# Gated decode step on one core: output weights in two halves with one transpose each, second feed-forward matrix ahead of the first keys

## Chip, cores and metric

The kernel runs on one core of one Trainium2 chip. The metric is device time in microseconds (us) of one execution: the median of the runs shown. The profile is of one further execution, whose span runs from its first to its last instruction.

## What is computed

One decode step for two sequences (B = 2, one token each, D = 640): attention of 32 heads over a cache of 4096 keys and values of 128 elements each, a feed-forward block with SiLU (F = 1728), and a sigmoid gate that mixes the two. All is float32.

```python
q = (x @ wq).reshape(B, 1, 32, 128).transpose(0, 2, 1, 3)
p = softmax(einsum("bhqd,bhkd->bhqk", q, k_cache) * 128 ** -0.5)
a = einsum("bhqk,bhkd->bhqd", p, v_cache).transpose(0, 2, 1, 3).reshape(B, 1, 4096) @ wo
b = silu(x @ w1) @ w2
g = sigmoid((x * gate_w).sum(-1, keepdims=True))
return g * a + (1 - g) * b
```

Keys and values are 134 MB each and everything else together is under 30 MB, so nearly all bytes that the kernel reads are read once, for one use.

## The kernel before

**Items and slabs.** The 32 heads are taken four at a time (Q = 4, HQ = 8 groups); a group and a sequence make an item, 16 in all. The keys of an item are one slab of 64 KB in each of 128 partitions (8.39 MB), its values another. Three slots of that size (`slabs`, line 52) hold everything large that is in flight: keys, values, query weights, feed-forward weights, output weights.

**Order of the loads.** `stream` (lines 80 to 88) is the list of slot contents in order: two blocks of weights (`wq` 0; `wq` 1, which also holds w1 and a few small inputs), then keys and values alternately. From item 7 on the keys of an item stand ahead of the values of the item before, because a block `mid` was put in after the keys of item 6. `mid` holds the output weights of groups 0 and 1 and the second feed-forward matrix; a last block `end` holds the output weights of groups 2 to 7. All these DMAs are issued by SP, in the order of the list. A block is issued when the block three places ahead of it has been marked as used up (`pump`, `spend`, lines 126 to 138); SP then waits until the engines have really read that slot. Everything that SP issues waits behind such a wait.

**One item.** `products` multiplies keys by the query, 60 of 128 columns of heads and positions on GpSimd (POOL, line 343), 68 on VectorE (DVE, line 346), in place. `scores` (line 354) sums over the 128 elements on DVE; after it the slot of the keys is spent. `peak` finds the maximum, `weights` (line 369, ScalarE) takes the exponential. One step later, beside the next item's keys, TensorE (PE) sums the weights (`total`), DVE inverts the sum (`invert`), and `values` (line 395) multiplies weights and values: 32 matmuls on four column strips, each recorded as two instructions, because the data are float32.

**From values to output.** `combine` (line 407) scales the result and keeps of each row the quarter that belongs to its head (`osb`, 128 x 4 x 128). A matmul with the 0/1 matrix `pick` (line 417) puts the rows of both sequences of a group in place in a PSUM tile `orow`. After the second sequence, `turn` (lines 425 to 429) sums over the four quarters (`row`) and transposes 128 x 128 elements to `oP`, four stationary operands for `project`. `project` (line 433) multiplies them by the group's output weights, four rows of 640 per partition. `accumulate` (line 222) has two targets: `early`, two strips of 320 columns, and `late`, four strips of 160; `merge` (line 235) copies `early` out on ScalarE and adds it into `late` with four small matmuls.

**Where the parts stand.** `middle` (line 443) runs after the values of item 5, on PE: the projections of groups 0 and 1 and `ffn_out`, with the contents of `mid`. Groups 2 to 7 are projected after the loop (line 474): 2 to 5 into `early`, 6 and 7 into `late`. The last values are loaded in two halves, and the last output weights in seven DMAs of which the last brings one row of 640 per partition. Then `ot` is copied (line 478) and written out by SP.

**Order on each engine.** The engines run their instructions in the order in which the program writes them (`manual_schedule`, line 60): nothing is moved by a scheduler. The loop is the one thing that sets it:

```python
for i in range(N + 1):
    if i < N:
        products(i)
    if i >= 1:
        total(i - 1); invert(i - 1); values(i - 1)
    if i == MID + 1:
        middle()
    if i < N:
        scores(i); peak(i); weights(i)
        ...
    if i >= 1:
        combine(i - 1)
        ...
```

Of the kernel before, what the change touches and what calls it, by code (L numbers as in the profile page):

```python
# [8 lines left out]
F32 = mybir.dt.float32  # L9
# [6 lines left out]
def tile_gated_decode(  # L16
# [12 lines left out]
    nc = tc.nc  # L29
# [18 lines left out]
    LEAD = 224  # L48
# [13 lines left out]

    ident = lead.tile([P, LEAD], F32, name="ident")[:, :P]

# [4 lines left out]
    MID = 5  # L69
# [5 lines left out]
    WO_MID = 2  # L75
    WO_AT = {}
    for grp in range(HQ):
        WO_AT[grp] = ("mid", W2T_AT + HD + grp * Q * D) if grp < WO_MID else ("end", (grp - WO_MID) * Q * D)
# [13 lines left out]

    def load_wo(grp, t):
        at = WO_AT[grp][1]
        src = wo[grp * QD : (grp + 1) * QD, :].rearrange("(p n) d -> p (n d)", n=Q)
        cuts = (0, Q * D - D, Q * D) if grp == HQ - 1 else (0, Q * D)
        for c0, c1 in zip(cuts, cuts[1:]):
            nc.sync.dma_start(t[:, at + c0 : at + c1], src[:, c0:c1])

    def load(what, n, t):  # L100
        if what in ("k", "v"):
# [3 lines left out]
            step = SLAB // 2 if (what, n) == ("v", N - 1) else SLAB  # L105
            for c in range(0, SLAB, step):
                nc.sync.dma_start(t[:, c : c + step], src[:, c : c + step])
# [7 lines left out]
        elif what == "mid":  # L115
            for grp in range(WO_MID):
                load_wo(grp, t)
# [4 lines left out]
        else:  # L122
            for grp in range(WO_MID, HQ):
                load_wo(grp, t)
# [33 lines left out]
    pick = const.tile([P, P + HB], F32, name="pick")  # L158
    nc.vector.memset(pick, 0.0)
    nc.vector.reduce_sum(pick[:, HB : P + HB : 32], sel.rearrange("p (q c) -> p q c", c=4), axis=AX.X)  # L160
# [9 lines left out]
    xz = const.tile([P, J, 32], F32, name="xz")  # L170
# [9 lines left out]
    hT = const.tile([P, FR, HB + 1], F32, name="hT")  # L180
# [35 lines left out]
    LAST = HQ - 2  # L216
# [3 lines left out]
    total_of = {"early": Q * LAST + FR + 1, "late": Q * (HQ - LAST) + 1}  # L220
# [66 lines left out]
    def ffn_out():  # L287
        t = T["mid", 0]
        for n in range(FR):
            accumulate(hT[:, n, :], t[:, n * D : (n + 1) * D])  # L290
# [8 lines left out]
        count["early"] += 1  # L299

# [103 lines left out]
    def combine(i):  # L404
        hq, b = items[i]
        osb = work.tile([P, 4, DH], F32, tag="osb", name="osb")
# [8 lines left out]
        if b == 0:  # L415
            PO[hq] = ps_r.tile([P, 4, DH], F32, name="orow")
        nc.tensor.matmul(  # L417
            PO[hq].rearrange("p c d -> p (c d)"),
            pick[:, HB * (1 - b) : HB * (1 - b) + P],
            osb.rearrange("p c d -> p (c d)"),  # L420
            start=(b == 0),
            stop=(b == B - 1),
        )

    def turn(hq):
        OP[hq] = const.tile([P, Q, 32], F32, name=f"oP{hq}")
        row = work.tile([P, DH], F32, name="row", bufs=1)
        nc.vector.reduce_sum(row, PO[hq].rearrange("p c d -> p d c"), axis=AX.X)  # L428
        nc.vector.transpose(OP[hq], row.rearrange("p (i n) -> p n i", n=Q))
# [3 lines left out]
    def project(grp):  # L433
        where, at = WO_AT[grp]
        w = T[where, 0][:, at : at + Q * D]
        to = "early" if grp < LAST else "late"
        for n in range(Q):
            lhsT = OP[grp][:, n, :] if count[to] == 0 else OP[grp][:, n, : HB + 1]
# [3 lines left out]

    def middle():
        for grp in range(WO_MID):
            project(grp)
# [57 lines left out]
```

## Time and profile before

| what | us |
|---|---|
| median of 3 runs | 700.46 |
| lowest and highest of them | 699.23, 700.59 |
| profiled execution | 700.36 |
| its span | 698.5 |
| DVE, POOL, PE busy | 469.4, 265.7, 224.7 |

Busy time is the sum of the durations of an engine's instructions; issuing DMAs is not counted. PE's time can be counted twice over where matmuls overlap, and PE's clock is granted between half and full speed. A page's lists give, for a group of instructions, the line of the kernel, the engine, what is written and read, the shape, the count, then busy time and mean duration, then the idle time of the engine ahead of them and what ended it. A timeline row is: start, duration, engine, line, operation, count, and in brackets the idle time ahead of it and its releaser. "SPq" is a DMA being issued, not being carried out; when it has landed shows in the time "to landing" or in the start of what waited for it.

### The profile page before, as it was taken

Reading aid. Unit: us, or ns where it says so; the run is one execution under the profiler, and the core shown is the slowest. Engines: PE = TensorE matmul, PEld = TensorE weight load, DVE = VectorE, ACT = ScalarE, POOL = GpSimd, SP = SyncE. Lnnn points to the kernel's source line nnn. Section 1 sums busy time; section 2 is a strip of 40 time slices with the busy share of each in tenths; the row PEclk is TensorE's granted clock in tenths of the full one; section 3 lists DMA queues with packets and bytes.
Section 4 is the critical chain, followed back from the end, with each engine's and each line's share of the span. In section 5 each row is a group of like instructions: output and inputs, shape, how many; then the busy total and the mean of one; then the engine's idle time right before and its main releaser. Section 6 shows DMA issues by size and latency. Waiting matters only on the chain.

```text
span 698.5 us, 3649 instructions
## 1 busy us (share of the span) xinstructions
PE 224.7 (32%) x1516; PEld 73.4 (11%) x1516; DVE 469.4 (67%) x215; ACT 37.8 (5%) x143; POOL 265.7 (38%) x27
## 2 busy tenths in 40 slices
PE   1630050605032150752240506050321406060477
PEld 1210010101010010210010102010100102010113
DVE  2016949394967869496949597695949495786901
ACT  0000000101010100101010101000010101010010
POOL 1006244270907153353618080624426080715300
PEclk9985565756657575877575757566565757566689
DMA  9999999999999999999999999999999999999995
GB/s 410 408 454 424 420 455 439 420 428 440 443 428 432 424 448 435 413 446 439 424 440 432 439 428 440 428 435 435 436 432 432 435 424 448 428 440 424 425 416 248
DMA packets 6803, 298.51 MB, mean 427 GB/s; under 512 B 759, under 2 KB 895, under 8 KB 1154
## 3 DMA queue, kind: packets, MB, share of 16 engines
q1 hardware_dynamic: 6780, 298.26, 98.8%
q8 instruction: 12, 0.20, 0.1%
q14 instruction: 5, 0.04, 0.0%
q10 hardware_dynamic: 6, 0.01, 0.0%
HBM read 298.26 MB, written 0.01 MB: 427 GB/s over the span
## 4 chain that ended last, share of the span: by engine, by line
DMA 60%; DVE 24%; PE 13%; another core or an unknown queue 1%; ACT 0%; issue 0%; SPq 0%; DVEq 0%; ACTq 0%
DMA k<-in_A_k_cache_dram 34%; DMA v<-in_A_v_cache_dram 20%; DVE s L354 15%; PE pv L395 10%; DVE k L346 8%; DMA wq<-in_B_w_dram 5%; PE acc L226 2%; PE orow L417 1%; PE hr L257 1%; DVE osb L407 0%; ACT pz L369 0%; PE tot L380 0%; DVE rg L388 0%; DVE m L359 0%
## 5 line engine op out<-in xcount | busy, mean ns | idle before, releaser
L343 POOL TENSOR_TENSOR k<-k,qsb 128x7680 f32<-128x7680 f32 x16 | 262.8, 16422 | 386.4 <-DMA k<-in_A_k_cache_dram 386.4
L354 DVE TENSOR_REDUCE s<-k 128x68 f32<-128x8704 f32 (+1 forms) x32 | 276.3, 8677 | 0.0
L346 DVE TENSOR_TENSOR k<-k,q 128x8704 f32<-128x8704 f32 x16 | 147.5, 9221 | 136.5 <-DMA k<-in_A_k_cache_dram 126.4
L395 PE MATMUL pv<-v,pz 128*32 128x512 f32 x1024 | 145.2, 730 | 247.9 <-DMA v<-in_A_v_cache_dram 247.9
L395 PEld LDWEIGHTS pv<-v,pz 128*32 128x32 f32 x1024 | 36.5, 131 | 342.7 <-issue 226.7
L417 PE MATMUL orow<-osb,pick 128*128 128x512 f32 x32 | 22.8, 800 | 117.4 <-DVE osb L407 117.4
L369 ACT ACTIVATE pz<-s,nb 32x128 f32<-32x128 f32 x64 | 25.5, 398 | 585.2 <-DVE nb L363 584.6
L407 DVE SCALAR_TENSOR_TENSOR osb<-pv,rg,own 128x512 f32<-128x512 f32 x16 | 12.0, 748 | 21.3 <-PE pv L395 21.2
L276 DVE STREAM_TRANSPOSE turned<-hr 128x416 f32<-128x416 f32 (+1 forms) x2 | 0.8, 414 | 29.4 <-PE hr L265 29.4
L380 PE MATMUL tot<-rs,fold 128*128 128x1 f32 x32 | 5.8, 251 | 43.9 <-ACT pz L369 43.9
L417 PEld LDWEIGHTS orow<-osb,pick 128*128 128x128 f32 x32 | 5.8, 226 | 127.1 <-DVE osb L407 127.1
L331 PE MATMUL q<-qrow,spread 128*128 128x128 f32 x32 | 7.2, 359 | 26.1 <-DVE tot L385 17.8
L314 PE MATMUL qr<-wq,xz 128*32 128x512 f32 x80 | 11.5, 745 | 8.7 <-DMA wq<-in_A_wq_dram 8.7
L428 DVE TENSOR_REDUCE row<-orow 128x128 f32<-128x512 f32 x8 | 5.5, 692 | 11.6 <-PE orow L417 11.6
L380 PEld LDWEIGHTS tot<-rs,fold 128*128 128x128 f32 x32 | 7.2, 235 | 55.3 <-ACT pz L369 52.3
L226 PE MATMUL acc<-mid,hT 128*17 128x320 f32 x52 | 10.0, 556 | 7.6 <-DMA mid<-in_B_w_dram 7.6
L369 ACT ACTIVATION_READ_ACCUMULATOR pz<-s,nb 32x1 f32 x64 | 11.8, 184 | 0.0
L226 PE MATMUL acc<-end,oP 128*17 128x320 f32 (+2 forms) x128 | 11.2, 367 | 0.0
L331 PEld LDWEIGHTS q<-qrow,spread 128*128 128x128 f32 x32 | 5.4, 240 | 33.0 <-issue 22.9
L478 DVE COPY ot<-acc 128x160 f32<-128x160 f32 x1 | 0.3, 324 | 11.0 <-PE acc L226 11.0
L257 PE MATMUL hr<-wq,xz 128*32 128x416 f32 x40 | 5.6, 681 | 3.7 <-DMA wq<-in_B_w_dram 3.7
L197 DVE COPY xz<-xT 128x10 f32<-128x10 f32 x1 | 0.2, 168 | 9.1 <-PE xT L189 9.1
(59 smaller groups left out, 69.0 us busy)
## 6 DMA issues: line engine op xcount, KB each, us to landing
v<-in_A_v_cache_dram SPq DMA_DIRECT2D x2, 4096.0 KB, 38.3
end<-in_A_wo_dram SPq DMA_DIRECT2D x5, 1280.0 KB, 21.3
wq<-in_B_w_dram SPq DMA_DIRECT2D x1, 4320.0 KB, 37.2
mid<-in_B_w_dram SPq DMA_DIRECT2D x1, 4160.0 KB, 26.8
mid<-in_A_wo_dram SPq DMA_DIRECT2D x2, 1280.0 KB, 17.4
wq<-in_A_wq_dram SPq DMA_DIRECT2D x1, 2048.0 KB, 26.5
end<-in_A_wo_dram SPq DMA_DIRECT2D x1, 960.0 KB, 27.0
end<-in_A_wo_dram SPq DMA_DIRECT2D x1, 320.0 KB, 27.3
```

The source lines that it names most:

```text
L226: nc.tensor.matmul(dst[32 * n : 32 * n + m, :], lhsT, w[:, n * width : (n + 1) * width], start=(count[to] == 0), stop=(count[to] == total_ ...
L257: nc.tensor.matmul(rows[32 * c : 32 * c + 32, :QF], xz[:, j, :], w[:, j, c * QF : (c + 1) * QF], start=(j == 0), stop=(j == J - 1),)
L314: nc.tensor.matmul(ps[u][32 * q : 32 * q + 32, :], xz[:, j, :], w[:, u * half : (u + 1) * half, q, :], start=(j == 0), stop=(j == J - 1),)
L331: nc.tensor.matmul(qps[hq][:, b, :], spread[:, b, :], qrow[:, hq, :], start=True, stop=True)
L343: nc.gpsimd.tensor_mul(k[:, CV:, :], k[:, CV:, :], qsb[hq][:, b, None, :].to_broadcast([P, C - CV, DH]))
L346: nc.vector.tensor_mul(k[:, :CV, :], k[:, :CV, :], qps[hq][:, b, None, :].to_broadcast([P, CV, DH]))
L354: nc.vector.reduce_sum(S[i][:, c0:c1], k[:, c0:c1, :], axis=AX.X)
L369: nc.scalar.activation(pz[i % 2][lo:hi, :, 4 * q : 4 * q + 4], S[i][lo:hi].rearrange("p (g c) -> p g c", c=4), AF.Exp, bias=M[i][lo:hi], s ...
L380: nc.tensor.matmul(t[:, :1], fold.rearrange("p a q c -> p (a q c)"), R[i], start=True, stop=True)
L395: nc.tensor.matmul(PV[i][32 * q : 32 * q + 32, :], pz[i % 2][:, gr, :], v[:, gr, :], start=(gr < 4), stop=(gr >= NG - 4),)
L407: nc.vector.scalar_tensor_tensor(osb, PV[i].rearrange("p (c d) -> p c d", d=DH), R[i], own[:, :, None].to_broadcast([P, 4, DH]), op0=ALU.mult,
L417: nc.tensor.matmul(PO[hq].rearrange("p c d -> p (c d)"), pick[:, HB * (1 - b) : HB * (1 - b) + P], osb.rearrange("p c d -> p (c d)"), star ...
```

## The change

- `w2`, the second feed-forward matrix, becomes a block of its own, third in the list, ahead of the first keys; `ffn_out` runs right after `ffn_in`. The blocks that follow come one place later in the rotation of three slots.
- The output weights become two blocks, `wo` 0 and 1, each half of them: 16 rows of 640 per partition (40 KB). `wo` 0 stands after the keys of item 9 (MID goes from 5 to 8) and is projected after the values of item 8, into `early`; `wo` 1 is the last block, in three DMAs of 8, 7 and 1 rows, and goes into `late`.
- The sum over the quarters moves into `combine`, ahead of the placing matmuls: each item does it once, from SBUF. Four matmuls of 128 columns then place its 32 rows in the half's PSUM tile, and `turn` transposes 128 x 512 elements from PSUM once per half.
- The last values are loaded in three cuts, a half and two quarters.
- The unused columns of `ident` go, and `xz` takes a place ahead of the slabs, which so start at another address. `hT` and `pick` change their layouts.

```diff
-    LEAD = 224
-    ident = lead.tile([P, LEAD], F32, name="ident")[:, :P]
+    ident = lead.tile([P, P], F32, name="ident")
+    xz = lead.tile([P, J, 32], F32, name="xz")
...
-    MID = 5
+    HG = HQ // 2
+    WR = HG * Q * DH // P
+    MID = HG * B
...
-    stream = [("wq", 0), ("wq", 1)]
+    stream = [("wq", 0), ("wq", 1), ("w2", 0)]
     for i in range(N):
         if i <= MID:
             stream += [("k", i), ("v", i)]
         elif i == MID + 1:
-            stream += [("k", i), ("mid", 0)]
+            stream += [("k", i), ("wo", 0)]
         else:
             stream += [("k", i), ("v", i - 1)]
-    stream += [("v", N - 1), ("end", 0)]
+    stream += [("v", N - 1), ("wo", 1)]
...
-            step = SLAB // 2 if (what, n) == ("v", N - 1) else SLAB
-            for c in range(0, SLAB, step):
-                nc.sync.dma_start(t[:, c : c + step], src[:, c : c + step])
+            cuts = (0, SLAB // 2, 3 * SLAB // 4, SLAB) if (what, n) == ("v", N - 1) else (0, SLAB)
+            for c0, c1 in zip(cuts, cuts[1:]):
+                nc.sync.dma_start(t[:, c0:c1], src[:, c0:c1])
...
-            for grp in range(WO_MID, HQ):
-                load_wo(grp, t)
+            src = wo[n * WR * P : (n + 1) * WR * P, :].rearrange("(p n) d -> p (n d)", n=WR)
+            cuts = (0, WR // 2, WR - 1, WR) if n == 1 else (0, WR)
+            for c0, c1 in zip(cuts, cuts[1:]):
+                nc.sync.dma_start(t[:, c0 * D : c1 * D], src[:, c0 * D : c1 * D])
...
-    total_of = {"early": Q * LAST + FR + 1, "late": Q * (HQ - LAST) + 1}
+    total_of = {"early": WR + FR + 1, "late": WR + 1}
...
     def combine(i):
         hq, b = items[i]
+        u, q = divmod(hq, HG)
...
-        if b == 0:
-            PO[hq] = ps_r.tile([P, 4, DH], F32, name="orow")
-        nc.tensor.matmul(
-            PO[hq].rearrange("p c d -> p (c d)"),
-            pick[:, HB * (1 - b) : HB * (1 - b) + P],
-            osb.rearrange("p c d -> p (c d)"),
-            start=(b == 0),
-            stop=(b == B - 1),
-        )
-
-    def turn(hq):
-        OP[hq] = const.tile([P, Q, 32], F32, name=f"oP{hq}")
         row = work.tile([P, DH], F32, name="row", bufs=1)
-        nc.vector.reduce_sum(row, PO[hq].rearrange("p c d -> p d c"), axis=AX.X)
-        nc.vector.transpose(OP[hq], row.rearrange("p (i n) -> p n i", n=Q))
+        nc.vector.reduce_sum(row, osb.rearrange("p c d -> p d c"), axis=AX.X)
+        if (q, b) == (0, 0):
+            PO[u] = ps_r.tile([P, Q, DH], F32, name="orow")
+        for h in range(Q):
+            nc.tensor.matmul(
+                PO[u][32 * q : 32 * q + 32, h, :],
+                pick[:, h, HB * (1 - b) : HB * (1 - b) + 32],
+                row,
+                start=(b == 0 and h == 0),
+                stop=(b == B - 1 and h == Q - 1),
+            )
+
+    def turn(u):
+        OP[u] = const.tile([P, WR, 32], F32, name=f"oP{u}")
+        nc.vector.transpose(OP[u], PO[u].rearrange("p h d -> p (h d)").rearrange("p (i n) -> p n i", n=WR))
...
     ffn_in()
+    ffn_out()
     for i in range(N + 1):
...
         if i == MID + 1:
-            middle()
+            project(0)
+            spend("wo", 0)
...
-            if items[i - 1][1] == B - 1:
-                turn(items[i - 1][0])
-    for grp in range(WO_MID, HQ):
-        project(grp)
+            if i % (HG * B) == 0:
+                turn(i // (HG * B) - 1)
+    project(1)
```

More of the change, by code (lines that the diff above doesn't have):

```diff
@@ L114, in load @@
                 nc.sync.dma_start(t[:, W1_AT : W1_AT + J * F], w1.rearrange("(p j) f -> p (j f)", j=J))
-        elif what == "mid":
-            for grp in range(WO_MID):
-                load_wo(grp, t)
+        elif what == "w2":
             nc.sync.dma_start(t[:, : FR * D], w2[:FM, :].rearrange("(p n) d -> p (n d)", n=FR))
@@ L441, in project @@
                 merge()
-    def middle():
-        for grp in range(WO_MID):
-            project(grp)
-        ffn_out()
-        spend("mid", 0)
     gates()
```

36 lines of the change are left out of this document (11 added, 25 removed).

## The prediction

> **What bounds the kernel now.** I read the page from the top: span, busy shares, slices (fortieths of the span), queue table.
>
> ```profile
> span 698.5 us, 3649 instructions
> ...
> PE 224.7 (32%) x1516; PEld 73.4 (11%) x1516; DVE 469.4 (67%) x215; ACT 37.8 (5%) x143; POOL 265.7 (38%) x27
> ...
> DMA  9999999999999999999999999999999999999995
> GB/s 410 408 454 424 420 455 439 420 428 440 443 428 432 424 448 435 413 446 439 424 440 432 439 428 440 428 435 435 436 432 432 435 424 448 428 440 424 425 416 248
> ...
> q1 hardware_dynamic: 6780, 298.26, 98.8%
> q8 instruction: 12, 0.20, 0.1%
> ```
>
> The DMA engines are busy in every slice but the last, where the stream ends; no compute engine passes 67%. SP's queue (q1) moved 298.26 MB and was busy 98.8% of the span. So three questions decide: does the stream move fewer bytes, does it run dry, and what stands behind its end? The timeline of DVE, and then that of all engines around the middle block, give the stream's pace (start us, duration, instruction, idle before it and releaser).
>
> ```profile
> 251.59 9.22 DVE L346 TENSOR_TENSOR k<-k,q 128x8704 f32<-128x8704 f32 x1 [6.79 <-DMA k<-in_A_k_cache_dram]
> ...
> 290.19 9.22 DVE L346 TENSOR_TENSOR k<-k,q 128x8704 f32<-128x8704 f32 x1 [10.14 <-issue]
> ```
>
> ```profile
> 293.19 2.35 PE L226 MATMUL acc<-mid,oP 128*32 128x320 f32 x16 [2.70 <-DMA mid<-in_A_wo_dram]
> 296.23 2.33 PE L226 MATMUL acc<-mid,oP 128*17 128x320 f32 x16 [0.69 <-DMA mid<-in_A_wo_dram]
> 306.18 9.98 PE L226 MATMUL acc<-mid,hT 128*17 128x320 f32 x52 [7.62 <-DMA mid<-in_B_w_dram]
> ...
> 316.96 0.33 SPq L107 DMA_DIRECT2D v<-in_A_v_cache_dram  x1
> ...
> 325.87 9.22 DVE L346 TENSOR_TENSOR k<-k,q 128x8704 f32<-128x8704 f32 x1 [4.87 <-DMA k<-in_A_k_cache_dram]
> ```
>
> L346 starts when its keys have landed. From 251.59 to 290.19, 38.60 us, a slab of values and one of keys landed, 2 x 8.39 MB (128 x 16384 x 4 bytes): 434.6 GB/s, or 19.3 us a slab. This pace is used below.
>
> The end is read from the chain of waits; the landing of the last weights from the seven issues of "end" (first and last start) and the time from issue to landing of the 320 KB one.
>
> ```profile
> 674.82 6.50 PE pv L395 x32
> ...
> 681.34 0.76 DVE osb L407
> ...
> 682.15 1.12 PE orow L417 x2
> 683.27 9.05 PE acc L226 x64
> ...
> 692.35 0.43 ACT part L237
> ...
> 692.82 0.46 PE acc L240 x8
> 693.29 2.07 PE acc L226 x56
> ...
> 695.45 0.32 DVE ot L478
> ```
>
> ```profile
> L98 SPq DMA_DIRECT2D end<-in_A_wo_dram x7: 327/418/441, 663.0 to 666.1; - x7
> ```
>
> ```profile
> end<-in_A_wo_dram SPq DMA_DIRECT2D x1, 320.0 KB, 27.3
> ```
>
> The last values land at 674.8, the last 320 KB of output weights at 666.1 + 27.3 = 693.4. PE works on to 695.36. Of these 2 us, 0.3 (the last row's 8 instructions at 2.07/56 = 0.037 us) always follow the landing. So a better tail alone can give 695.36 - 693.7 = 1.7 us at most.
>
> **The change part by part.** The profiled execution took 700.36 us, 1.86 more than its span; the median of the runs shown is 700.46. I sum against 700.36.
>
> *Bytes: 0.* The same tensors are read once.
>
> *Start of the stream.* The second matrix (4.42 MB, 10.2 us) is issued where the first keys were; these now wait for the slot of the first query weights, which frees where the first values are issued now (32.85), and the values for the next slot (44.62).
>
> ```profile
> 32.85 0.33 SPq L107 DMA_DIRECT2D v<-in_A_v_cache_dram  x1
> 38.90 1.61 PE L257 MATMUL hr<-wq,xz 128*32 128x416 f32 x8 [3.74 <-DMA wq<-in_B_w_dram]
> ...
> 44.62 0.33 SPq L107 DMA_DIRECT2D k<-in_A_k_cache_dram  x1
> ...
> 47.75 0.37 DVE L285 TENSOR_SCALAR hTh<-hTt,half 128x17 f32<-128x17 f32 x2
> ...
> 58.18 9.22 DVE L346 TENSOR_TENSOR k<-k,q 128x8704 f32<-128x8704 f32 x1 [10.06 <-DMA k<-in_A_k_cache_dram]
> ```
>
> W1 lands at 38.9, so w2 at 49.1: keys 0, issued at 32.9, have 16 us of cover, values 0 (44.6) have until 68.4. Keys 1 need w2 spent: hTh is ready at 48.1, the 56 matmul instructions take 9.98 us and a little more, so about 60, with cover until 87.7. Behind ffn_out's new wait on PE stand only total(0) and values(0), which need scores of keys landing at 68.4. Cost 0; uncovered, each late microsecond of an issue would cost one.
>
> *Middle.* SP issues values 9 once keys 9 are spent. Before, the like place is keys 6: landed 290.19, values issued at 316.96, 26.8 later; the queue held mid and keys 7 until 325.87, a cushion of 8.9 us. Now the block is 5.24 MB instead of 7.04, 4.1 us shorter: 4.8 us remain. Still positive: 0. project(0) makes PE wait for wo half 0; behind it stand the query, orow and total matmuls, which wait for DVE's scores anyway. Its slot is spent some 12 us (64 instructions; 9.98 for 52 above) after that landing, long before its keys are due.
>
> *DVE and PE.* DVE gets 8 more row sums and two large transposes for eight small ones; PE turns 32 orow instructions into 128 and gains 32 in the projections (fewer rows go to the two-wide accumulator). DVE waits 4.9 to 10 us for each of the keys quoted, so 0.7 us an item is hidden. The 1516 matmul instructions become 1644, so q8's 12 fetches of 16 KB become about 13: 0 to 0.6 us (16 KB at 434.6/16 GB/s) on one of 16 engines. I take 0.
>
> *Cuts.* Output weights go in 4 DMAs with rows of 2.5 to 40 KB instead of 9 with mostly 10 KB rows; the last values in 3 instead of 2. In mid, two groups (2.62 MB) landed from 290.19 to 296.23, 6.04 us against 6.03 at the pace: no loss. In the tail 7.86 MB took 693.4 - 674.8 = 18.6 against 18.1: a loss of 0.5. The gain is between 0 and 0.5; I take 0.2, so the last landing is at 693.2. The slabs' start moves by (288 - 224) x 4 = 256 bytes; no row shows a start's effect, all slices together run from 408 to 455 GB/s, and I take 0.
>
> The Trainium skill, SBUF — State Buffer, "The DMA setup-cost knee", gives every DMA a roughly fixed 2 us beside its bytes. By that, 1.31 MB would need an estimated 5.0 us, and four DMAs fewer would save 8 us (692.4). The trace disagrees: the second group landed 296.23 - 293.19 = 3.04 us after the first.
>
> *Tail.* Backward from 693.2 at the pace: the seven-row cut lands 0.75 earlier, 692.45; the eight-row cut 5.28 before that, 687.2; the last quarter of values 6.03 before, 681.1 (the end block is 2.62 MB smaller, so the values land 6 us later). What PE costs depends on its granted clock, the next-to-last number of a window's row ahead of DMA share and GB/s.
>
> ```profile
> 660.00:670.00 10.00, 9.13 (x84) 2.87 (x76) 5.05 (x8) 1.96 (x8) 0.00 (x0) 1.00 1.01 437
> 670.00:680.00 10.00, 5.71 (x36) 1.25 (x32) 0.00 (x0) 0.00 (x0) 0.00 (x0) 0.68 0.95 403
> ```
>
> ```profile
> 666.89 3.64 PE L395 MATMUL pv<-v,pz 128*32 128x512 f32 x32
> 674.82 6.44 PE L395 MATMUL pv<-v,pz 128*32 128x512 f32 x32 [4.29 <-DMA v<-in_A_v_cache_dram]
> ```
>
> ```profile
> L428 DVE TENSOR_REDUCE row<-orow 128x128 f32<-128x512 f32 x8 | 5.5, 692 | 11.6 <-PE orow L417 11.6
> L429 DVE STREAM_TRANSPOSE oP<-row 128x128 f32<-128x128 f32 x8 | 3.2, 405 | 0.3
> L276 DVE STREAM_TRANSPOSE turned<-hr 128x416 f32<-128x416 f32 x1 | 0.6, 618 | 29.4 <-PE hr L265 29.4
> ```
>
> The same 32 instructions take 3.64 us at full clock and 6.44 after 4.29 us of waiting. The last quarter's 16 take 1.8 (3.2 slow); osb 0.76; the row sum 0.69; orow's eight 128-column instructions between the 1.12 of today's pair (the same columns) and twice that, I take 1.4; the 128x512 transpose, at the slope from 405 ns (128 columns) to 618 (416), 0.7; gaps 0.2. Sum 5.6: ready at 686.7, before the eight-row cut (687.2). Its 64 instructions and merge's 8 take 72 x 0.037 = 2.7, to 689.9. PE then waits 2.5 us for the seven-row cut (692.45): 56 instructions 2.07, the last row 0.3: 694.8 at full clock, 0.5 us before now. At half clock these 64 take 4.7: 697.2, 1.8 us after now.
>
> The grant decides. From 679 to 692.45 PE has 1.8 + 1.4 + 2.7 = 5.9 us of work in 13.5 us. The 670 to 680 row, 5.71 busy of 10, was granted 0.68; the 660 to 670 row, 9.13 busy, 1.00. I take the middle, 0.84: 2.37/0.84 = 2.8, end at 695.3.
>
> The Trainium skill, TensorE: Matmul & The Clock Gate, Part 1, says that PE falls to half clock after an idle window of about 3.4 us and needs about as long of steady work to return. By the rule, waits of 2.5 us can cost nothing (699.8). The trace agrees for the 4.29 us wait; it quotes none of 2.5.
>
> Sum: 700.36 + (695.3 - 695.36) = **700.3 us**: one wait of the tail is traded for another.
>
> **The rivals.**
>
> *A, PE cold in the last cuts (slower).* The wait for the seven-row cut, after a thinly filled stretch, drops the clock, and 64 instructions run at half rate behind the stream: 700.36 + 1.8 = 702.2. It decides where PE ends 696.8 or later. For it: 0.68 in the window quoted. Against: no single wait reaches 4.29 us. 15%.
>
> *B, the stream runs dry (slower).* If values 9 are issued over 4.8 us later than I work out, each further microsecond is lost; the one price in the trace is the difference of the cushions, 4.1 us: 704.5. Against: DVE's 26.8 us from landing to spent holds no new work ahead of spend. 3%.
>
> *C, the stream gets denser (faster).* After 58.18, 23.3 MB were landed; the other 274.96 MB took 635.2 us, against 632.7 at the pace: 2.5 us were lost somewhere, part of it perhaps to DMA boundaries and short rows. Were 1.5 of it regained, with a warm PE: 700.36 - 1.5 - 0.5 = 698.4; all of it, 697.4. Against: the two mid groups ran at the pace. This case also holds the fixed price per DMA (692.4). 12%.
>
> *D, the change does not shorten the chain.* If orow and the transposes cost twice my numbers, they still end near the eight-row landing: inside the forecast.
>
> **How the numbers follow.** The forecast has 70%: 699.2 (warm PE, 0.5 instead of 0.2 for the cuts, 0.3 less than today's tail elsewhere) to 701.8. A 15%, B 3%, C 12%. The range of 8 in 10 leaves out B, most of C and the far end of A: 699.0 to 702.2. About 0.2%, 1.4 us, is what a measurement of this kernel can tell from no change: faster than 699.06 is C, 12%; slower than 701.86 is A and B, 18%; within, 70%.
>
> **What would show it.** Right: the DMA slices stay at 9 to the last, w2 lands near 49, the last cut near 693 of the span, orow and transpose end before the eight-row cut, and PE's last 64 instructions take 2.4 to 3.5 us behind the seven-row cut. Wrong: a slice under 9 around the output half in the middle (B); these 64 instructions near 4.7 us under a clock near 0.5 (A); a last landing before 692 (C); a later last landing by more than 0.6, which would mean that the order of the stream or the slabs' start cost what I took at nothing.

## The result and the profile after

The changed kernel takes 701.28 us (median of 22 runs, 700.46 to 702.86), the kernel before 700.16 beside it (22 runs, 699.20 to 700.90). The ratio is 1.0022, with a 95% interval of 1.0016 to 1.0028: slower by 1.1 us in the medians and by 1.5 us by the ratio, where no change was forecast. The profiled execution of the changed kernel took 701.61 us with a span of 699.8, 1.3 us more than the span of before.

The page of the changed kernel first: span, DMA share in 40 slices, queues.

```profile
span 699.8 us, 3906 instructions
...
DMA  9999999999999999999999999999999999999994
...
q1 hardware_dynamic: 6204, 298.26, 98.6%
q8 instruction: 13, 0.21, 0.1%
```

The bytes are the same, the stream has no gap, and it does not end later. The list of DMA issues gives the last 320 KB (kilobytes, us from issue to landing); the lines of L115 give the start of the last issue, 670.4.

```profile
wo<-in_A_wo_dram SPq DMA_DIRECT2D x1, 320.0 KB, 23.0
```

```profile
L115 SPq DMA_DIRECT2D wo<-in_A_wo_dram x4: 328/328/441, 404.7 to 670.4; - x4
```

670.4 + 23.0 is 693.4, as before. So the 1.3 us arise behind the stream. The timeline of PE and DVE shows the tail (start, duration, engine, line, shape, count, idle time ahead and its releaser):

```profile
681.04 1.92 PE L385 MATMUL pv<-v,pz 128*32 128x512 f32 x16 [0.95 <-DMA v<-in_A_v_cache_dram]
684.89 1.06 PE L411 MATMUL orow<-row,pick 128*32 128x128 f32 x8 [1.93 <-DVE row L407]
687.54 0.72 PE L215 MATMUL acc<-wo,oP 128*32 128x160 f32 x8 [1.59 <-DMA wo<-in_A_wo_dram]
688.77 0.73 PE L229 MATMUL acc<-part,ident 64*17 64x160 f32 x8 [0.52 <-ACT part L226]
689.43 6.71 PE L215 MATMUL acc<-wo,oP 128*17 128x160 f32 x120
```

```profile
683.03 0.75 DVE L398 SCALAR_TENSOR_TENSOR osb<-pv,rg,own 128x512 f32<-128x512 f32 x1 [7.76 <-PE pv L385]
683.82 1.02 DVE L407 TENSOR_REDUCE row<-osb 128x128 f32<-128x512 f32 x1
685.99 0.72 DVE L421 STREAM_TRANSPOSE oP<-orow 128x512 f32<-128x512 f32 x1 [1.15 <-PE orow L411]
696.29 0.32 DVE L464 COPY ot<-acc 128x160 f32<-128x160 f32 x1 [9.59 <-PE acc L215]
```

The 120 instructions of the last row group have no bracket: PE waits for no cut after 687.54. They take 6.71 us, 56 ns each, where the last 56 of before took 37. The stretches of the same trace say why (window, its length, then busy time and count of PE, PEld, DVE, ACT, POOL, then the granted clock, DMA share, GB/s; the last four rows show PE alone):

```profile
680.00:687.00 7.00, 3.07 (x28) 1.21 (x24) 2.48 (x3) 0.00 (x0) 0.00 (x0) 1.00 0.97 416
687.00:694.00 7.00, 5.95 (x88) 3.27 (x92) 0.00 (x0) 0.42 (x1) 0.00 (x0) 0.55 0.57 241
```

```profile
684.23:687.64 3.41, 1.16 (x12) 1.00 1.00 428
687.65:691.06 3.41, 2.89 (x44) 0.50 0.86 363
691.06:694.47 3.41, 3.41 (x56) 0.50 0.15 58
694.47:697.00 2.53, 1.68 (x48) 1.00 0.00 0
```

From 680 to 687 PE worked 3.07 of 7 us, in pieces with 0.95, 1.93 and 1.59 us of idle time ahead of them. From 687.65 to 694.47 its clock stood at half; on both sides it was full. The traces of this case have only these two values, and the clock changes at borders that lie 3.41 us apart; a figure between 0.50 and 1.00 is a mean over a window. In the 3.41 us ahead of the fall PE was busy for 1.16 us, in those ahead of the return for all 3.41. DVE's copy of `ot` starts at 696.29, against 695.45 before: +0.84.

The other 0.46 of the 1.30 lie behind that copy: 3.51 us from its start to the span's end, 3.05 before (0.49 with the spans unrounded, 699.83 and 698.50). SP's waits (us in total, times, longest) show where; the first row is of before, the second of after.

```profile
SPq L499 <- PEq L499: 0.6, 2, 0.4
```

```profile
SPq L485 <- PEq L485: 1.1, 2, 0.9
```

This is SP in the exchange of signals in which all engines end the program. The records of GpSimd show it as the late one: from the start of its last signal to that of its DRAIN are 0.41 us, and the DRAIN takes 0.23; before, both take 0.08. The trace of before has 75 records of GpSimd's, that of after 73.

### The profile page after: what moved, and what is told of

It reads as the page before. It is cut to its first block, busy times and chain, and to the rows that moved or that the text cites. A ratio compares the mean times of both kernels' runs of the same rounds, so it can differ in the third digit from the quotient of the medians.

```text
span 699.8 us, 3906 instructions
## 1 busy us (share of the span) xinstructions
PE 223.2 (32%) x1644; PEld 85.7 (12%) x1644; DVE 478.2 (68%) x217; ACT 37.8 (5%) x143; POOL 265.5 (38%) x27
## 3 DMA queue, kind: packets, MB, share of 16 engines
q1 hardware_dynamic: 6204, 298.26, 98.6%
## 4 chain that ended last, share of the span: by engine, by line
DMA 59%; DVE 28%; PE 11%; issue 0%; SPq 0%; ACT 0%; DVEq 0%
DMA k<-in_A_k_cache_dram 42%; DVE s L344 17%; DVE k L336 9%; DMA v<-in_A_v_cache_dram 8%; PE pv L385 7%; DMA w<-in_B_w_dram 7%; DMA wo<-in_A_wo_dram 3%; PE acc L215 2%; PE orow L411 1%; DVE row L407 1%; DVE osb L398 0%; PE tot L370 0%; DVE rg L378 0%; DVE m L349 0%; DVE m L351 0%
## 5 line engine op out<-in xcount | busy, mean ns | idle before, releaser
L385 PE MATMUL pv<-v,pz 128*32 128x512 f32 x1024 | 137.7, 697 | 150.8 <-DMA v<-in_A_v_cache_dram 150.8
L411 PE MATMUL orow<-row,pick 128*32 128x128 f32 x128 | 25.0, 361 | 207.7 <-DVE row L407 207.7
L411 PEld LDWEIGHTS orow<-row,pick 128*32 128x32 f32 x128 | 16.8, 143 | 219.7 <-DVE row L407 210.9
L215 PE MATMUL acc<-wo,oP 128*17 128x160 f32 (+2 forms) x192 | 17.7, 433 | 12.7 <-DMA wo<-in_A_wo_dram 12.7
L370 PE MATMUL tot<-rs,fold 128*128 128x1 f32 x32 | 8.4, 331 | 40.2 <-ACT pz L359 40.2
L407 DVE TENSOR_REDUCE row<-osb 128x128 f32<-128x512 f32 x16 | 16.3, 1019 | 0.6
L304 PE MATMUL qr<-wq,xz 128*32 128x512 f32 x80 | 10.1, 663 | 8.9 <-DMA wq<-in_A_wq_dram 8.9
L215 PEld LDWEIGHTS acc<-wo,oP 128*17 128x17 f32 (+1 forms) x192 | 8.4, 121 | 22.2 <-issue 18.3
L215 PE MATMUL acc<-w,hT 128*17 128x320 f32 (+1 forms) x52 | 8.9, 509 | 4.2 <-DMA w<-in_B_w_dram 4.2
```

Source lines behind the costliest of these rows:

```text
L215: nc.tensor.matmul(dst[32 * n : 32 * n + m, :], lhsT, w[:, n * width : (n + 1) * width], start=(count[to] == 0), stop=(count[to] == total_ ...
L304: nc.tensor.matmul(ps[u][32 * q : 32 * q + 32, :], xz[:, j, :], w[:, u * half : (u + 1) * half, q, :], start=(j == 0), stop=(j == J - 1),)
L370: nc.tensor.matmul(t[:, :1], fold.rearrange("p a q c -> p (a q c)"), R[i], start=True, stop=True)
L385: nc.tensor.matmul(PV[i][32 * q : 32 * q + 32, :], pz[i % 2][:, gr, :], v[:, gr, :], start=(gr < 4), stop=(gr >= NG - 4),)
L407: nc.vector.reduce_sum(row, osb.rearrange("p c d -> p d c"), axis=AX.X)
L411: nc.tensor.matmul(PO[u][32 * q : 32 * q + 32, h, :], pick[:, h, HB * (1 - b) : HB * (1 - b) + 32], row, start=(b == 0 and h == 0), stop=( ...
```

## The experiments

Theory 1: PE's clock falls in the thin stretch before 687, and PE, not the stream, sets the end. 1b: `merge` adds to it, since its copy of `early` on ScalarE waits for the first row of `late` and PE stands 0.5 us for it. Theory 2, a rival: the slabs' other address costs something. Theory 3, another: the large last cuts make PE wait. Theory 4: the end of GpSimd's program costs 0.46. Theory 5: the new order of the stream is free, and what matters is only that less is left behind the last values (12.4 us in place of 18.6). Every kernel was timed beside the kernel before, whose medians there were 699.46 to 700.22, so rows are compared by their ratios. PE's end is read from the start of the `ot` copy; this start and the span are of one profiled execution each.

| edit | `ot` starts | span | median (runs) | ratio to before, 95% |
|---|---|---|---|---|
| after: spare matmuls | 695.27 | 698.8 | 700.93 (11) | 1.0016 [1.0007, 1.0025] |
| after: seven cuts | 695.27 | 698.8 | 701.37 (11) | 1.0020 [1.0010, 1.0030] |
| after: early copy | 695.38 | 698.9 | 700.52 (11) | 1.0006 [0.9997, 1.0015] |
| after: slabs' address | 696.23 | 699.8 | 701.66 (11) | 1.0022 [1.0013, 1.0032] |
| after: two memsets | 696.01 | 699.1 | 701.23 (11) | 1.0023 [1.0014, 1.0032] |
| after: copy, memsets | 695.12 | 698.2 | 700.18 (11) | 1.0006 [0.9997, 1.0015] |
| after: matmuls, copy, memsets | 694.81 | 697.9 | 699.81 (11) | 1.0003 [0.9994, 1.0012] |
| the same, seven cuts | 693.98 | 697.1 | 698.91 (11) | 0.9990 [0.9981, 0.9999] |
| after: matmuls, copy | 695.03 | 698.6 | 700.45 (11) | 1.0007 [0.9998, 1.0016] |
| the same, four memsets | 694.90 | 698.0 | 699.95 (11) | 1.0002 [0.9993, 1.0010] |
| before: order of after | 697.06 | 700.6 | 702.62 (5) | 1.0038 [1.0025, 1.0050] |
| before: w2 first, small middle | 695.75 | 699.1 | 700.81 (11) | 1.0010 [1.0002, 1.0019] |
| before: spare matmuls | 694.04 | 697.1 | 699.02 (11) | 0.9994 [0.9985, 1.0002] |

### Spare matmuls in the thin stretch

`spin` is a matmul of `ones` (128 x 128) with 512 columns of the query rows into a PSUM tile that nobody reads.

```diff
+    def spin(n):
+        t = ps_s.tile([P, 512], F32, tag="sm", name="spin")
+        for _ in range(n):
+            nc.tensor.matmul(t, ones, qrow[:, 0:4, :], start=True, stop=True)
...
+            if u == 1 and n == WR // 2 - 1:
+                spin(2)
...
+        if i == N:
+            spin(2)
         if i >= 1:
             combine(i - 1)
...
+    spin(1)
     project(1)
```

> The changed kernel with five more matmuls (constants into a spare PSUM tile that nobody reads) in PE's waits of the tail: two after the last values, one after the last placing matmuls, two between row 8 and row 9 of the last output weights. Nothing else differs. Theory 1 (PE's clock falls to half in the thinly filled stretch before the last output weights land, and the last 128 + 8 instructions then run behind the stream): the clock stays at 1.00 after 687, the last projection ends 0.6 to 1.3 us earlier than in the changed kernel, near 695.1, which is the landing of the seven-row cut (692.7) plus 2.07 plus 0.3; about 700.2 us. Theory 2 (the stream itself lands later, by order, by the slabs' start or by the cuts): no change, 701.3. Theory 3 (the waits for the cuts hold PE up, whatever its clock): no change or slower by the added matmuls.

The timeline of PE and one stretch:

```profile
687.42 0.48 PE L215 MATMUL acc<-wo,oP 128*32 128x160 f32 x8 [0.16 <-DMA wo<-in_A_wo_dram]
688.43 0.46 PE L229 MATMUL acc<-part,ident 64*17 64x160 f32 x8 [0.53 <-ACT part L226]
688.82 2.10 PE L215 MATMUL acc<-wo,oP 128*17 128x160 f32 x56
...
692.76 2.37 PE L215 MATMUL acc<-wo,oP 128*17 128x160 f32 x64
```

```profile
687.00:694.00 7.00, 6.31 (x114) 3.62 (x117) 0.00 (x0) 0.42 (x1) 0.00 (x0) 1.00 0.58 241
```

With more work PE ends 1.0 us earlier in the trace: the clock is 1.00, 56 instructions take 2.10 us, the last 64 take 2.37. The idle half microsecond before `merge` remains and costs nothing here, since PE reaches the seven-row cut about when it lands. The runs don't show the gain by themselves: the ratio 1.0016 and that of the changed kernel, 1.0022, have intervals that overlap, and 4 of the 11 runs took 701.65 us or more. The profiled execution, 700.60, is one of the faster ones; what happened in the four, no record shows.

### Seven cuts

```diff
-            cuts = (0, WR // 2, WR - 1, WR) if n == 1 else (0, WR)
+            cuts = (0, 4, 8, 10, 12, 14, 15, 16) if n == 1 else (0, WR)
```

> The changed kernel with the last output weights in seven cuts (4, 4, 2, 2, 2, 1, 1 rows) instead of three (8, 7, 1). Theory 1 (cold PE): PE starts its last projection when the transpose is done, 686.7, and not at 687.5, and is then bound by its own clock: 0.5 to 1.0 us less than the changed kernel, 700.3 to 700.8, and the wait for the cuts behind row 4 is zero. Theory 3 (the wait for the seven-row cut, as the prediction had it): PE follows the stream row by row and ends 0.3 to 0.6 us after the last landing at 693.5, so 2.0 to 2.4 us less, 699.0 to 699.3. Theory 2 (stream): no change, or 4 more DMAs make it slower.

```profile
686.78 0.76 PE L215 MATMUL acc<-wo,oP 128*32 128x160 f32 x8 [0.81 <-DVE oP L421]
...
688.74 6.38 PE L215 MATMUL acc<-wo,oP 128*17 128x160 f32 x120
```

The first cut now lands before the operand is ready: PE waits for DVE's transpose, starts 0.76 us earlier, and still works through most of the 120 instructions at half clock (0.56 from 687 to 694) without waiting for any cut. It ends 1.0 us earlier in this trace, but the profiled execution is one of the faster ones (700.58, with runs from 699.83 to 702.85), and the median does not move. Theory 3 is wrong for the changed kernel as it stands: to an engine that lags behind the cuts, smaller ones give nothing that the medians show.

### The early sums copied in the middle

```diff
+    part = const.tile([64, W2], F32, name="part")
     def merge():
-        part = const.tile([64, W2], F32, name="part")
-        nc.scalar.copy(part, early[:64, :])
...
             spend("wo", 0)
+            nc.scalar.copy(part, early[:64, :])
```

> The changed kernel with the ScalarE copy of the early sums made right after the first output half has been projected, in the middle of the run, and not between row 1 and row 2 of the last half. Theory 1 (PE is bound by its own work from 687.5 on): the 0.5 us in which PE waits for that copy goes, and little else: 0.4 to 1.0 us less, 700.3 to 700.9. Theory 3 (PE waits for the seven-row cut at 692.7 anyway): no change. Theory 2 (stream): no change.

```profile
688.13 0.73 PE L229 MATMUL acc<-part,ident 64*17 64x160 f32 x8
688.80 3.43 PE L215 MATMUL acc<-wo,oP 128*17 128x160 f32 x56
692.95 2.37 PE L215 MATMUL acc<-wo,oP 128*17 128x160 f32 x64 [0.72 <-DMA wo<-in_A_wo_dram]
```

```profile
687.00:694.00 7.00, 5.56 (x104) 3.39 (x108) 0.23 (x1) 0.00 (x0) 0.00 (x0) 0.76 0.58 247
```

The first 56 instructions still run slowly (3.43 us), but unbroken and earlier, and PE is done 0.72 us before the seven-row cut; the last 64 run at full clock. In the medians this is the largest single gain: ratio 1.0006 against 1.0020 to 1.0022 of the two kernels beside it that keep the late copy and have no spare matmuls. So 1b holds, though not by its own half microsecond alone. The stretches between the borders show how:

```profile
684.75:688.16 3.41, 1.50 (x20) 1.00 1.00 429
688.17:691.58 3.41, 3.41 (x55) 0.50 0.76 318
```

The clock falls here too, but the first 3.41 us at half clock hold no idle time, and full clock returns after them. In the four profiles with the late copy and without spare matmuls PE was busy for 2.37 to 2.89 us of the first stretch at half clock, with the wait for the copy (0.52 to 0.54 us) in it, and the clock stayed at half for a second one, 6.83 us in all. There is one profile of each kernel.

### The slabs' address

```diff
     ident = lead.tile([P, P], F32, name="ident")
-    xz = lead.tile([P, J, 32], F32, name="xz")
+    hTh = lead.tile([P, 2, HB + 1], F32, name="hTh")
+    hTt = lead.tile([P, 1, HB + 1], F32, name="hTt")
+    sel = lead.tile([P, 4 * Q], F32, name="sel")
+    own = lead.tile([P, 4], F32, name="own")
+    half = lead.tile([P, 2], F32, name="half")
```

> The changed kernel with the slabs starting at the same address as in the kernel before (small tiles fill the 896 bytes ahead of them, xz goes behind). Theory 2 in the form of the slabs' start: 1.0 us less, 700.2. Theories 1 and 3: no change, 701.0 to 701.5, stream ends at 693.5 as before.

1.0022 again, and the same tail (the 120 instructions take 7.00 us). The address is free.

### Two more memsets on GpSimd

```diff
     nc.gpsimd.memset(hTt, 0.0)
+    nc.gpsimd.memset(hTt, 0.0)
+    nc.gpsimd.memset(hTt, 0.0)
```

> The changed kernel with two more tiny memsets on GpSimd in the first microseconds (hTt is cleared three times instead of once), so that GpSimd has as many instructions as in the kernel before. Theory 4 (part of the loss, 0.46 us of the span, lies behind the output: SP's last wait for the other engines is 1.1 us against 0.6 before, because GpSimd's instruction stream ends at another place and its last instructions come late): that wait goes back to about 0.6 and the time falls by 0.3 to 0.6 us, to 700.7 to 701.0. Theory 1 alone (all of it is PE's cold tail): no change, 701.3.

```profile
SPq L487 <- PEq L487: 0.6, 2, 0.4
```

The wait at the end is back at 0.6, and 3.09 us lie behind the start of the `ot` copy in place of 3.51: two instructions more, 0.4 us less. The median doesn't show it (1.0023): these runs spread over 2.3 us (700.54 to 702.83), and the clock goes with it: its mean over the whole run is 0.659 to 0.662 in the four slowest, 0.665 to 0.668 in the others.

### Copy and memsets together

The two edits above in one kernel.

> The changed kernel with two edits that were tried one by one: the early copy of the sums and two more memsets on GpSimd. Theory 1 and theory 4 together (independent terms): the gains add up, 0.8 less for the copy (700.52 against 701.28) and 0.45 for GpSimd: 700.0 to 700.3, no longer slower than the kernel before. If GpSimd's end is no term of its own: 700.5.

```profile
684.80:688.21 3.41, 1.78 (x24) 1.00 0.99 426
```

In its profile the clock did not fall at all, though the stretch from 680 to 687 was as thin as ever (3.40 of 7 us busy): the 56 instructions take 2.10 us, PE waits 2.30 for the seven-row cut, and `ot` starts at 695.12. The borders lie elsewhere. The 3.41 us ahead of the one that matters take in the first row and `merge`, 1.78 us of work, where the five profiles in which the clock fell have 1.06 to 1.52. From the start of the last placing matmuls to that border it is 3.18 us here, 2.76 in the changed kernel, 1.96 with two memsets, 1.37 with seven cuts: the borders are not tied to the tail, so whether one as thin as this goes cold can be luck; how often it does, one profile of each kernel can't say. One stretch alone is no rule either: 1.49 us of work from 670.58 to 673.99 in the changed kernel, behind a full stretch, left the clock at 1.00.

The median, 700.18, lies 0.4 above the kernel before beside it (699.77), and the interval holds no change. The ratio, 1.0006, is that of the early copy alone, so the memsets don't show in it.

### The kernel before with the order of after

```diff
-    MID = 5
-    WO_MID = 2
+    MID = 8
+    WO_MID = 4
...
-    stream = [("wq", 0), ("wq", 1)]
+    stream = [("wq", 0), ("wq", 1), ("w2", 0)]
```

`w2` is a block of its own and `ffn_out` follows `ffn_in`; the output weights stay in groups, four in the middle, four at the end. Not shown here: `hT` has the layout of the changed kernel, and a few small tiles stand ahead of the slabs in place of the unused columns of `ident`, so that the slabs keep their address.

> The kernel before with the order of loads of the changed one: the second feed-forward matrix third in the list and used at once, the output weights of groups 0 to 3 after the keys of item 9, groups 4 to 7 at the end; a transpose per group, one matmul per item for orow, the last values in halves and the last weights in cuts of a group, as before. The slabs start where they did. Theory 2 (the early matrix or the place of the middle block costs the stream something): the last landing is later than 693.5 by the loss. Theory 5 (the stream is the same, but the last block is 2.62 MB smaller, so the values land 6.0 us later before its end, and everything that PE does after the last values has 12.4 us of cover instead of 18.6): last landing at 693.5, PE ends at 697 to 699 (values 6.4 cold, osb 0.8, orow 1.1, two groups into the early sums 4.3, merge 1.4, 2.1 behind it), 702 to 704 us.

```profile
681.52 5.66 PE L397 MATMUL pv<-v,pz 128*32 128x512 f32 x32 [4.75 <-DMA v<-in_A_v_cache_dram]
...
689.12 4.76 PE L227 MATMUL acc<-end,oP 128*17 128x320 f32 x40
...
694.83 2.10 PE L227 MATMUL acc<-end,oP 128*17 128x160 f32 x56
```

The last landing stays where it was (22.3 us from issue, 693.7), so the order is free for the stream. But the last values now come 6.7 us later, PE takes 5.66 us for them after a wait of 4.75, the projections begin at 689.1, and `merge` and the last 56 instructions run wholly behind the stream. With the longer end of GpSimd's program (1.1 here too) the kernel is slower by 0.38%: without the three cuts of the last values and the other layouts, the new order alone costs more than the whole change (0.22%).

### w2 first, with a small block in the middle

```diff
-    stream = [("wq", 0), ("wq", 1)]
+    stream = [("wq", 0), ("wq", 1), ("w2", 0)]
```

The kernel before with `w2` ahead of the first keys, and `mid` reduced to the two groups (2.62 MB), MID still 5. This was meant to make the stream run dry in the middle.

> As the run before it, but with the middle block kept after the keys of item 6 and holding the output weights of groups 0 and 1 alone (2.62 MB); groups 2 to 7 at the end as in the kernel before. The cushion by which the next values are issued before the stream runs dry was worked out as 8.9 us with 7.04 MB and 4.7 with 5.24 MB; with 2.62 MB it is 6.03 + 19.3 - 26.8 = -1.5 us. Theory of the cushion: the stream stops once, for 1.5 us and the time from issue to first packet (1 to 2 us), the last landing moves to 695 to 697, and with PE's tail as before, 2.0 to 3.5 us more than before: 702.2 to 703.7. If the queue held other work (no cushion needed): 700.2.

```profile
309.15 0.33 SPq L112 DMA_DIRECT2D v<-in_A_v_cache_dram  x1
```

It did not run dry: the values were issued at 309.15, when `mid` was spent, 18 us ahead of the end of the scores (327.5), behind which I had expected them. So the run says nothing on how small a cushion may be; that stays open. What it shows is that an early `w2` costs the stream nothing: its last landing is at 693.6 as well. The kernel is slower by 0.10% all the same (interval 1.0002 to 1.0019); in its profile `ot` starts 0.30 us later than before, and 0.3 us more lie behind it.

### All three costs taken away

Spare matmuls (two, one, two), the early copy, and two memsets, in the changed kernel.

> The changed kernel with the three suspected costs removed together: spare matmuls (two after the last values, one after the last placing matmuls, two between row 8 and row 9 of the last projection), the copy of the early sums made right after the first half of the output weights, and two more small GpSimd memsets at the start. Theory 1 (PE's granted clock) with 1b (merge waits for its copy) and 4 (the end of GpSimd's program): the clock shows 1.00 in all windows from 670, PE's 64 instructions start at the landing of the seven-row cut (692.6) and PE ends near 695.1, the time from SP's wait to the end is back at 0.6, the span is 698.2 to 698.7 and the median 0.1% to 0.2% under the changed kernel's, so at that of the kernel before (ratio 0.9995 to 1.001). Rival (the rest of the loss lies in the stream): the ratio stays at 1.002.

```profile
687.96 2.10 PE L217 MATMUL acc<-wo,oP 128*17 128x160 f32 x56
689.99 1.98 PE L430 MATMUL spin<-qrow,ones 128*128 128x512 f32 x4
692.37 2.37 PE L217 MATMUL acc<-wo,oP 128*17 128x160 f32 x64 [0.40 <-DMA wo<-in_A_wo_dram]
```

Ratio 1.0003, and all 11 runs lie within 0.42 us (699.61 to 700.03), where the changed kernel's spread over 2.4: these costs make up the loss, as far as the interval can tell.

### The same with seven cuts

The kernel above with the seven cuts, and without the two spare matmuls between rows 8 and 9.

> As the run with all three costs removed, but with the last output weights in seven cuts (4, 4, 2, 2, 2, 1, 1 rows) and without the two spare matmuls between rows 8 and 9. With a warm PE the size of the cuts should matter for the first time: PE follows the landings two rows at a time, only the last row's 8 instructions stand behind the end of the stream, and PE ends at 693.9 to 694.2, 1.4 us before the kernel before; ratio 0.997 to 0.999. Rival (each further DMA costs the stream something at its end, or PE goes cold between the cuts): PE ends at 695 or later, ratio 1.000 to 1.002.

```profile
687.87 3.18 PE L217 MATMUL acc<-wo,oP 128*17 128x160 f32 x88
691.82 1.30 PE L217 MATMUL acc<-wo,oP 128*17 128x160 f32 x24 [0.77 <-DMA wo<-in_A_wo_dram]
693.44 0.47 PE L217 MATMUL acc<-wo,oP 128*17 128x160 f32 x8 [0.32 <-DMA wo<-in_A_wo_dram]
```

Now PE waits for the cuts, and only the last row stands behind the stream: 698.91 us, 0.10% under the kernel before (interval 0.9981 to 0.9999). The cuts that gave nothing in the medians to a cold PE give 0.9 us to a warm one (699.81 to 698.91).

### The kernel before with spare matmuls

```diff
         for gr in range(NG):
+            if i == N - 1 and gr == NG // 2:
+                spin(4)
```

> The kernel before with four spare matmuls between the two halves of its last values, in the wait of 4.29 us. Theory 1 holds for the kernel before as well: the last 32 instructions of pv take 3.64 us in place of 6.44, the projections follow the landings of the groups, and PE ends near 693.9 in place of 695.36; the median falls by 0.7 to 1.7 us (ratio 0.9975 to 0.999), and the runs spread less. Rival (the wait for the stream sets the end whatever the clock): the ratio stays within 0.0005 of 1.

```profile
670.56 3.70 PE L409 MATMUL spin<-qrow,ones 128*128 128x512 f32 x8
675.00 3.64 PE L397 MATMUL pv<-v,pz 128*32 128x512 f32 x32 [0.74 <-DMA v<-in_A_v_cache_dram]
```

The last values take 3.64 us in place of 6.44, and `ot` starts at 694.04, 1.4 us earlier than in the profile of before. The median fell by 0.44 only, under the 0.7 that I had expected, and the interval holds no change: many runs of before on that chip were near 699.3 anyway. It is as fast as the best version of the changed kernel beside it (699.02 and 698.91). So the halves themselves gain nothing that these runs can show; what moved PE's end in this profile is the clock.

### GpSimd's end with a steady clock

Two kernels timed beside each other, both with spare matmuls and the early copy; the second has four more memsets. The two expectations count one GpSimd instruction more than the trace has records (73 and 77).

> The changed kernel with spare matmuls (two, one, two) and the early copy, but without further memsets on GpSimd: 74 GpSimd instructions in all, as in the changed kernel. PE keeps its clock, so the runs should spread by a few tenths of a microsecond only, and what the end of GpSimd's program costs can be read from the medians. Theory 4 (the end of GpSimd's program): SP's last wait takes 1.1, PE ends near 695.1 and the median lies 0.4 to 0.5 us above that of the kernel with four more memsets beside it in this call. Rival (the longer wait at the end is inside the span but not in the device time): both medians agree within 0.2 us.

> The same kernel with four more small GpSimd memsets at the start, 78 GpSimd instructions in all (the kernel before has 76, the changed one 74). Theory 4, where it is the number of instructions as such (few enough and the end comes late): the last wait takes 0.6, and the median is 0.4 to 0.5 us under that of the kernel with 74. Rival (it is where the last instructions fall, and 76 happens to be a good place): the last wait is 0.9 to 1.1 again with 78, and the medians agree within 0.2 us.

SP's last wait, first of the kernel without memsets, then with four:

```profile
SPq L496 <- PEq L496: 1.1, 2, 0.9
```

```profile
SPq L500 <- PEq L500: 0.6, 2, 0.4
```

The medians are 700.45 and 699.95 us, the fastest runs 700.29 and 699.69: the half microsecond is part of the device time, though 4 of the 11 runs with memsets took 700.45 or more. With 75 and 77 records the end is short, with 73 it is long; with 72 (`w2` first, small middle) the wait was 0.9. The traces settle which of the two theories holds, by GpSimd's 69th record. With 72 or 73 records a pause of 0.36 to 0.42 us stands ahead of it. With 73 it is the DRAIN at the end, with 72 the record behind this DRAIN. With 77 it is another DRAIN at 642.67, ahead of the last product, where 0.40 us lie in place of 0.07 and nothing at the end waits for them; with 75 it falls into a wait of 38 us or more, where a pause can't be seen. So it goes by the place in GpSimd's program, and not by the number of instructions as such. What the engine does in the pause, no record shows.

## Why the prediction was wrong

The measured 701.28 us lies inside the band of 699.2 to 701.8 that the forecast had, but what it said was no change, and the interval of the ratio, 1.0016 to 1.0028, holds only slower ones.

*Bytes, Start of the stream* held: `w2` was used at 48.87 (49.1 was said), and no slice of the DMA share is under 9 before the last. So did *Middle*: the timeline of DVE shows keys 10 starting with a cushion of 4.7 us behind the issue of values 9 at 443.31 (4.8 was said).

```profile
445.02 1.02 DVE L407 TENSOR_REDUCE row<-osb 128x128 f32<-128x512 f32 x1
447.99 9.22 DVE L336 TENSOR_TENSOR k<-k,q 128x8704 f32<-128x8704 f32 x1 [1.95 <-DMA k<-in_A_k_cache_dram]
```

DVE still waited 1.95 us there, so rival B did not come about.

*Cuts* took 0.2 us of gain; there was none (last landing 693.4). Three, five or seven DMAs at the end, another address and another order all left the last landing at 693.1 to 693.7. Rival C is out.

*Tail* came out right up to 686.7, by two errors that cancelled: the row sum from SBUF took 1.02 us (0.69 was taken from the one out of PSUM), the eight placing instructions 1.06 (1.4 was taken). The eight-row cut came 0.3 late. Then the step that failed: "The grant decides ... I take the middle, 0.84". The clock has no middle: it was half from 687.65 to 694.47 and full after that. I had applied 0.84 to the last 64 instructions only and kept "72 x 0.037 = 2.7" for the eight-row cut. That stretch took about 5.6 us: 0.72 for the first row, 0.52 of waiting for ScalarE, 0.73 for `merge`, and 3.7 for 56 instructions (the 57th of the 120 starts at 693.15) that take 2.10 with a warm PE. So PE was not back for the seven-row cut with 2.5 us to spare. This cut was forecast for 692.45 and landed at 692.7; PE got to it at 693.15, and ended 0.8 later than the 695.3 of the forecast. The last 64 instructions took 3.0 us, near the 2.8 of the sum and inside the 2.4 to 3.5 named as a sign of being right. That was luck: they ran the first 1.3 us at half clock and the rest at full. The wait behind `merge` stood in no term of the sum.

The figure for a warm PE was good: 694.8 forecast; the three kernels with spare matmuls and the early copy and with the seven-row cut end between 694.7 and 695.0.

Rival A had the right mechanism, 15%, and a wrong trigger and price. The clock fell not in the wait for the seven-row cut, which never took place, but behind the waits of 0.95, 1.93 and 1.59 us before it. My argument against A, that no single wait reaches 4.29 us, was the wrong test: the clock fell behind a stretch of 3.41 us in which PE was busy for 1.16 us, and the like stretch with spare matmuls, 3.2 us or more, held the clock. The spare matmuls shorten the waits as well, so the runs don't separate the share of work from the length of the waits. The price in this execution was half of A's 1.8. Four of the 22 runs, at 702.38 to 702.86, lie near the 702.2 of A. That the clock was lower still in their tails is not shown: one execution alone has a profile, and the mean clock over the whole run, which set the slowest runs with two memsets apart, doesn't do so here (0.664 in the four, 0.661 to 0.668 in the others).

The Trainium skill, TensorE: Matmul & The Clock Gate, "HAM oscillation — how this bites in real kernels", puts the rule as no idle gap of PE over about 3.4 us. By it nothing would have been lost here, and the trace differs: the longest idle time between 681 and 689 was 1.93 us. The next section of that page, "A second HAM failure mode: psum-queue depth-cycling", says of another kernel that short but frequent idle times between groups of matmuls make the clock swing between half and full; the fall behind the stretch from 680 to 687 agrees with that. Part 1 of the page says that the window that is watched runs freely and does not start with the kernel. The traces agree: the borders are 3.41 us apart, and from the last placing matmuls to the next one that matters it is 1.37 to 3.18 us. How far the times of the runs spread doesn't follow from this alone: 2.4 us in the changed kernel, 1.7 in the kernel before, and 0.42 to 1.58 in the kernels with spare matmuls.

The remaining 0.46 us, the end of GpSimd's program, had no step in the prediction. I had looked at GpSimd's work, which the change leaves alone, and not at its two instructions fewer. By the ratios, clock and copy took about 1.05 us (1.0022 to 1.0007) and GpSimd's end 0.35 (1.0007 to 1.0002; 0.50 in the medians): together 1.4 of the 1.5 us lost. The intervals are wider than GpSimd's part, and in two other pairs, the changed kernel and the one with the early copy, each with and without two memsets, the ratio doesn't show it. For this part the traces and the one pair with a steady clock speak.

## What to carry to other kernels

Where a chain of small matmuls ends a kernel behind a stream, ask how much of each few microseconds PE is busy, not only for its longest wait: here 1.06 to 1.52 us of work in 3.41 were followed by half clock in five profiles of the changed kernel and its variants. Then look for waits in the first microseconds at half clock, since here they went with a second 3.41 us of it: a copy moved out of the way, together with spare matmuls in the gaps, took back most of the loss. Cut the last transfer finely only once the engine behind it keeps up; the same cuts were worth nothing in the medians to a cold PE and 0.9 us to a warm one. A change of a fifth of a per cent has to be looked for behind the last output too.

## What was not expected of the hardware

Two GpSimd instructions fewer lengthened the end of the program by about half a microsecond, and two or four trivial ones brought it back, because a pause of about 0.4 us keeps its place in GpSimd's program. A row sum over a strided view took 1019 ns from SBUF (16 times) where the same shape took 692 from PSUM:

```profile
L407 DVE TENSOR_REDUCE row<-osb 128x128 f32<-128x512 f32 x16 | 16.3, 1019 | 0.6
```

And the stream did not care about anything that was done to it: with 6204 or 6780 packets, rows of 2.5 or 40 KB, and another start of the slabs, the last bytes landed within 0.6 us of one another (693.1 to 693.7).
